# Batch 0 of a fused attention kernel: its first 256 tokens with 256 keys side by side, new first fetches, and a new order

## The chip, the cores and the metric

The kernel runs on one core of one Trainium2 chip. The metric is the device time of one execution in microseconds (us). Three runs of the kernel before took 471.76, 472.86 and 473.77 us; the median is 472.86. Lower is better.

The engines of a core are named as in the profile: PE is TensorE with its matmuls and PEld its weight loads, DVE is VectorE, ACT is ScalarE, POOL is GpSimd, and SP is the engine that does nothing here but issue transfers (DMAs). Each engine takes its own list of instructions in order; between engines there are semaphores.

## The reference

Two attentions stand one behind the other. The first has 8 heads of 64, a causal window of 128 keys and a bias that falls with the distance; its output, 512 wide, is the input of a mixture of four attention experts, of which each token uses the two with the highest gate.

```python
# q, k, v: (8 batches, 8 heads, 576 tokens, 64)
rel = pos[:, None] - pos[None, :]
bias = slopes[:, None, None] * (-np.abs(rel))
mask = (rel >= 0) & (rel < 128)
scores = np.where(mask, q @ k.T / 8 + bias, -1e9)
x = (softmax(scores) @ v)              # -> (8, 576, 512)

logits = x @ w_gate                    # 4 experts, the best two of each token
for e in range(4):
    q, k, v = x @ wq[e], x @ wk[e], x @ wv[e]
    a = softmax(causal(q @ k.T / 8))   # full causal, 576 x 576
    out += (weight of e) * (a @ v @ wo[e])
```

## The kernel before

**Tiling.** Tokens stand in blocks of 128 (four, and a tail of 64), heads in pairs. A batch has four pairs; `g` counts pairs over all batches, so batch 0 has g = 0 to 3. For a pair the first attention computes scores with the tokens on partitions (`products`, L435), adds the bias table `tbt` and takes the row's minimum of the negated scores in one DVE instruction (`softmax_block`, L288; in the trace CUSTOM_DVE_ANT_0, in the order below ISA), takes the exponential with a running sum on ACT (`exp_block`, L292), divides by the sum on POOL or ACT (`normalise`, L470: a reduce and a reciprocal on DVE and one scaling for each block), transposes the probabilities on PE (`half_t`, L511), copies them from PSUM (`evac`, L261, or `split`, L559) and multiplies them with the values (`half_pv`, L534).

**The wrap.** Block 0 has 128 keys. Every later block sees 256 keys, of which each row uses 128 in a staircase. So its scores are computed as two halves of 64 rows with 192 keys each, and `wrap` (L457, COPY_PREDICATED on DVE) folds them into 128 columns: where the mask `mkt` is set, the score of the key 128 places further on replaces the one that the row doesn't use. After the transposes `split` multiplies the folded probabilities with the two masks of `tmt` and so lays them out for 256 keys again.

**Halves of batch 0.** At the start nothing is there to overlap with, so the four pairs of batch 0 are done in halves (`half_units`, L1121): x = 0 is the first 256 tokens (blocks 0 and 1) of all four pairs, x = 1 the rest. `fetch` (L328) brings q and k of the first 256 tokens of a pair (two transfers of 128 KB, one for each half of the partitions, into tiles named w_90 and w_91 in the lists below), and later the rest; `fetch_v` (L360) brings the values `vt`. All of these are issued by SP. The tables `tbt`, `idt` (identity for transposes), `tmt` and `mkt` are issued by ACT (L1094 to L1098).

**The mixture.** Its matmuls keep accuracy by splitting each operand into a rounded part and a rest: weights WH and WL, inputs xT as a high and a low tile. `wload` (L931) fetches a chunk `in_wall` of 772 columns, `wprep` (L946) rounds it to WH (POOL) and subtracts to WL (DVE or POOL); `vproj` (L665) and `qkproj` (L734) do three matmuls for each of four chunks: high x high, high x WL, low x WH. In the trace these are the matmuls with `wx,WH`, `wx,WL` and `WH,wx`; `wx` tiles hold the first attention's output, four of them for batch 0, one per pair.

**Order and buffers.** No code line runs at once: every call is recorded in a list. `plan` (L199) puts the list in the order that a table of numbers (`ORDER`, L38) gives, which also chooses between alternatives (ACT or DVE for a copy, POOL or ACT for a scaling, DVE or POOL for a subtraction) and inserts filler matmuls on a zero tile (`QJm`). `place` (L158) then gives each tile a buffer from its pool. So all instructions have the line of the last loop, L1189, in the trace, and tiles appear by buffer: `w` and `wx` in SBUF, `ps` in PSUM. A copy out of PSUM, for example, is recorded with both engines as alternatives:

```python
    def evac(dst, src, n=0):
        nc.any(("scalar", "copy", (dst, src), None), ("vector", "tensor_copy", (dst, src), None))
```

The program starts at L1093: zero tile, the first table, `fetch(0, 1, 0)`, the other tables, then pairs 1 to 3, the values and the weights.

## Time and profile before

| | |
|---|---|
| median of three runs | 472.86 us |
| the profiled execution | 473.2 us, its span 471.4 us |
| granted clock of PE, mean | 0.998 |
| PE busy | 462.7 us (98% of the span) |
| PEld, DVE, ACT, POOL busy | 403.8, 409.3, 370.5, 222.7 us |
| transferred | 44.99 MB, 95 GB/s over the span |
| chain of waits that ended last | PE 84%, DMA 5%, SP's issues 3%, DVE 3%, ACT 2% |

How to read it: a share is an average over stages. PE is busy nearly all the time, so elsewhere than at the start (and at the end) another engine matters only where PE waits for it. PE's busy time contains the filler matmuls, which do no work for the result. A list entry of a float32 matmul appears twice in PE's timeline, since it runs in two passes; one of the rounded type appears once.

### The profile page before, as it was taken

The numbers are of one execution on the slowest core, as the hardware profiler recorded it, in microseconds if no ns is written. First come the engines' busy times: TensorE is split into PE (matmuls) and PEld (weight loads), VectorE is DVE, ScalarE is ACT, GpSimd is POOL, SyncE is SP. The second block draws the span as 40 slices with busy tenths as digits, with TensorE's granted clock in tenths as the row PEclk, the third lists the DMA queues.
The fourth block names the chain that finished last, engine by engine and source line by source line (L and its number), as shares of the span: only waits on it lengthen the run. The fifth ranks groups of instructions, "written<-read, shape, count | busy, mean of one in ns | idle before, by whom it ended". The sixth has DMA issues, their size and how long they took to land.

```text
span 471.4 us, 17542 instructions
## 1 busy us (share of the span) xinstructions
PE 462.7 (98%) x6380; PEld 403.8 (86%) x6380; DVE 409.3 (87%) x1894; ACT 370.5 (79%) x1409; POOL 222.7 (47%) x464
## 2 busy tenths in 40 slices
PE   7999999999999999999999999999999999999996
PEld 5788999897889789797898987898789897899775
DVE  6999999979998998879989798798999979966852
ACT  5968879989978688796989798897976959833952
POOL 4833968183916346261470907426263623561430
PEclk9999999999999999999999999999999999999999
DMA  7899410345320653150441281602731030300033
GB/s 202 266 221 246 112 52 1 77 103 141 108 80 0 139 142 117 29 140 1 115 129 37 80 189 39 180 2 61 205 121 38 3 86 2 120 1 1 3 113 112
DMA packets 29862, 44.99 MB, mean 95 GB/s; under 512 B 9424, under 2 KB 15824, under 8 KB 29776
## 3 DMA queue, kind: packets, MB, share of 16 engines
q1 hardware_dynamic: 29040, 43.42, 34.0%
q8 instruction: 50, 0.82, 0.8%
q10 hardware_dynamic: 736, 0.46, 0.4%
q14 instruction: 36, 0.29, 0.2%
HBM read 34.42 MB, written 9.44 MB: 93 GB/s over the span
## 4 chain that ended last, share of the span: by engine, by line
PE 84%; DMA 5%; SPq 3%; DVE 3%; ACT 2%; POOL 1%; issue 1%; DVEq 0%
PE ps L1189 84%; DMA w<-in_hd 4%; SPq L1189 3%; DVE w L1189 2%; ACT w L1189 2%; POOL w L1189 1%; DMA w<-in_wall 1%; DVE ps L1189 1%; DVE WL L1189 0%; DVE ALm L1189 0%; ACT AHm L1189 0%; DVE mr L1189 0%; DVE nm L1189 0%; POOL QJm L1189 0%; DVE ALTm L1189 0%
## 5 line engine op out<-in xcount | busy, mean ns | idle before, releaser
L1189 ACT COPY w<-ps 128x256 f32<-128x256 f32 (+2 forms) x232 | 92.4, 443 | 29.8 <-PE ps L1189 21.3
L1189 PE MATMUL ps<-wx,WH 128*128 128x288 f32 (+2 forms) x512 | 110.4, 300 | 0.0
L1189 ACT ACTIVATE w<-w,nm 128x128 f32<-128x128 f32 x252 | 98.9, 397 | 7.3 <-DVE nm L1189 5.8
L1189 POOL TENSOR_SCALAR w<-w,mr,w 128x256 f32<-128x256 f32 (+3 forms) x128 | 78.2, 622 | 43.2 <-DVE mr L1189 24.1
L1189 POOL TENSOR_SCALAR w<-w,r 128x128 f32<-128x128 f32 x177 | 64.6, 378 | 68.3 <-PE ps L1189 25.4
L1189 PEld LDWEIGHTS ps<-wx,WH 128*128 128x128 f32 x512 | 83.2, 190 | 1.5 <-issue 0.3
L1189 ACT ACTIVATE w<-w,mnm 128x512 f32<-128x512 f32 (+3 forms) x128 | 71.2, 558 | 10.0 <-DVE mnm L1189 9.4
L1189 DVE TENSOR_TENSOR w<-ps,tmt 128x768 f32<-128x768 f32 (+3 forms) x96 | 72.5, 770 | 3.3 <-PE ps L1189 2.2
L1189 DVE CUSTOM_DVE_ANT_0 w<-ps,tbt 128x128 f32<-128x128 f32 x288 | 71.7, 283 | 1.1
L1189 PE MATMUL ps<-wx,WL 128*128 128x288 f32 (+2 forms) x256 | 71.9, 298 | 0.0
L1189 PE MATMUL ps<-WH,wx 128*128 128x260 f32 x288 | 61.5, 285 | 0.0
L1189 PE MATMUL ps<-w 64*64 64x192 f32 (+3 forms) x1256 | 58.6, 304 | 2.3 <-DMA w<-in_hd 1.7
L1189 PE MATMUL ps<-idt,w 64*128 64x64 f32 (+1 forms) x1152 | 58.6, 230 | 1.0 <-POOL w L1189 0.9
L1189 PEld LDWEIGHTS ps<-idt,w 64*128 64x128 f32 (+1 forms) x1152 | 47.4, 139 | 11.0 <-issue 3.4
L1189 PE MATMUL ps<-w,vt 64*64 64x192 f32 (+3 forms) x1344 | 56.3, 283 | 0.0
L1189 PEld LDWEIGHTS ps<-w,vt 64*64 64x64 f32 (+1 forms) x1344 | 50.0, 133 | 5.7 <-DVE r L1189 0.6
L1189 DVE COPY_PREDICATED ps<-mkt,ps 128x128 f32<-128x128 int32 (+2 forms) x160 | 49.2, 329 | 5.4 <-PE ps L1189 5.0
L1189 PEld LDWEIGHTS ps<-w 64*64 64x64 f32 (+1 forms) x1256 | 44.0, 134 | 8.6 <-DMA w<-in_hd 2.7
L1189 DVE CUSTOM_DVE_ANT_0 w<-ps,mtt 128x256 f32<-128x256 f32 (+2 forms) x96 | 49.8, 551 | 0.8 <-PE ps L1189 0.4
L1189 PEld LDWEIGHTS ps<-WH,wx 128*128 128x128 f32 x288 | 48.0, 189 | 0.8 <-issue 0.3
L1189 ACT ACTIVATION_READ_ACCUMULATOR w<-w,nm 128x1 f32 x252 | 48.6, 193 | 0.0
L1189 PE MATMUL ps<-w,w 128*64 128x64 f32 (+4 forms) x576 | 48.0, 319 | 0.0
(111 smaller groups left out, 947.5 us busy)
## 6 DMA issues: line engine op xcount, KB each, us to landing
w<-in_hd SPq DMA_DIRECT2D x56, 288.0 KB, 4.6
vt<-in_vd SPq DMA_DIRECT2D x28, 320.0 KB, 3.7
out<-w SPq DMA_DIRECT2D x31, 256.0 KB, 2.5
w<-in_hd SPq DMA_DIRECT2D x14, 128.0 KB, 3.5
w<-in_hd SPq DMA_DIRECT2D x56, 32.0 KB, 3.7
w<-in_wall SPq DMA_DIRECT2D x4, 386.0 KB, 6.6
out<-w SPq DMA_DIRECT2D x8, 128.0 KB, 3.3
vt<-in_vd SPq DMA_DIRECT2D x4, 192.0 KB, 3.8
```

The source lines that it names most:

```text
L1189: getattr(getattr(tc.nc, e), m)(*a, **k)
```

## The change

The change does six things, all in batch 0, and then gives a new order table.

1. **First 256 tokens without the wrap.** For x = 0, `first_blocks` computes block 0 with 128 keys and block 1 with 256 keys side by side (matmuls of 128 and 256 columns instead of 128 and 192), one softmax instruction of 128 and one of 256 columns, and one exp of each for a head. There is no COPY_PREDICATED. The bias comes from a new table `FT` with a causal part and the part for the 128 keys before; it lies in the buffer `KKm`, which the mixture uses only later, and is made from `tbt` by two DVE and four POOL operations. `first_norm` scales the two widths. `half_t` makes six transposes for a pair instead of four and copies them in two plain copies of 384 columns, without `split`; each pair has its own buffers.
2. **First fetches on two queues.** The two first transfers of all four pairs are now recorded first of all, one on SP and one on ACT.
3. **Tables later.** `tmt` and `mkt[:, P:]` move from ACT to SP, recorded behind the weight chunks.
4. **Weights in pieces.** `wprep` rounds and subtracts each of the four chunks in two pieces of 512 and 260 columns.
5. **Low weights last.** In the first half of batch 0's projections (`terms`) the four WL matmuls of an accumulation come behind the eight with WH.
6. **A new `ORDER`**, nearly every number of it. It is the one that also moves work in the rest of the program, transfers on SP among it. Its rows say nothing to a reader, so only a line of each stands here.

The filler matmuls go from 16 to 14. The last loop is L1213 in the changed kernel.

```diff
-    "c-pmi4OAT2b!Jz++w~r*8dX`{p6;D)A8^2i7{-v$Ss23%*pPq+){p}Z*f0SHZ192&4rIZB2_%p}299A2UKB$tIZ`ZqL;{W&ix?*0fCDFJ1`@Oj8`u>yQY<"
+    "c-pmC4^(7Vd7t<0H*@duUNSG4m&~Ly%EZA!!zfs2K_P-d3uZ8of&~j6IEA>R5aEP1V4*?<1!XH(IAznNvIb6<(_IB!n%&CklCoy0;DHDgDi}z?LWN|hOT$"
...
     def fetch(g, m, x):
...
-            for x in range(g, g + m):
-                a = hd[0, NP_ - 1 - x]
...
-                for j in range(2):
...
-                    nc.sync.dma_start(v2[D * j : D * j + D, 1 - x % 2, :, :n], src)
+            for j, e in enumerate((nc.sync, nc.scalar)):
...
+                e.dma_start(v2[D * j : D * j + D, z, :, :n], src)
...
+    def first_blocks(g, ss, q, k, tb):
+        nm, sm, pt = state[g, 0]
+        for i in range(2):
+            n = P + P * i
+            for h in range(2):
+                d = slice(D * h, D * h + D)
+                for y in range(2):
+                    m = P * i + D * y
+                    nc.tensor.matmul(
+                        ss[h][D * y : D * y + D, P * i : P * i + n], q[h][d, m : m + D], k[d, :n], start=True, stop=True
+                    )
+        for h in range(2):
+            for i in range(2):
...
+                softmax_block(a, v, bias, nm[:, c : c + 1], P + P * i)
+                exp_block(None, v, nm[:, c : c + 1], sm[:, c, 0:1], P + P * i)
+
+    def first_norm(g):
...
+            scl(v, v, r[:, c : c + 1])
...
     def half_t(g, x):
...
-            evac(w[:, : 4 * P].rearrange("p (h n) -> p h n", h=2)[:, :, :P], t[:, 0:2, :], 2 * P)
-            split(diag_pair(w, 1, 1, P), t[:, 2:4, :], P)
+            for h in range(2):
+                t = ps_t.tile([P, 4, P], F32, tag="t", name=f"tA{g}_{h}")
+                for k in range(3):
+                    nc.tensor.transpose(t[:, k, :], pt[:, 3 * h + k, :], idt)
+                evac(w[:, 3 * P * h : 3 * P * h + 3 * P].rearrange("p (a n) -> p a n", n=P), t[:, :3, :])
...
+    def terms(late):
+        return sorted(((c, j) for c in range(4) for j in range(3)), key=lambda z: late and z[1] == 2)
...
     def wprep(c):
         if c < 4:
...
+            for f in (slice(0, 4 * P), slice(4 * P, NW)):
+                w, hi, lo = wst[c][:, f], WH[:, NP_ - 1 - c, f], WL[:, NP_ - 1 - c, f]
+                rnd(hi, w)
+                ssub(lo, w, hi.bitcast(F32))
+            return
...
-    fetch(0, 1, 0)
+    for g in range(4):
+        fetch(g, 1, 0)
     nc.scalar.dma_start(idt, ident)
-    nc.scalar.dma_start(tmt, tm)
-    nc.scalar.dma_start(mkt[:, P:], mk[:, P:])
...
+    nc.vector.tensor_scalar(FT[:, 3, :, 0, :], tbt[:, 3, 0:3:2], -1.0e6, NEG, op0=ALU.is_ge, op1=mul)
+    nc.vector.tensor_tensor(FT[:, 3, :, 0, :], FT[:, 3, :, 0, :].bitcast(F32), tbt[:, 3, 1:4:2], add)
+    nc.gpsimd.tensor_scalar(FT[:, 3, :, 1, :], tbt[:, 3, 0:3:2], 1.0, 0.0, op0=mul, op1=add)
+    for p in (2, 1, 0):
+        nc.gpsimd.tensor_scalar(FT[:, p], FT[:, 3].bitcast(F32), float(4 ** (3 - p)), 0.0, op0=mul, op1=add)
...
     for c in range(1, 4):
         wload(c)
+    nc.sync.dma_start(tmt, tm)
+    nc.sync.dma_start(mkt[:, P:], mk[:, P:])
```

Three places of the lists follow, before and then after.

**ACT at the start**, from its first instruction. `hd` is the input with q and k, ACT_TABLE_LOAD loads the table for exp, and an ACTIVATE is an exp of one block.

```order
L1189 DMA tbt<-in_tb 128x640
L1189 DMA idt<-in_ident 128x128
L1189 DMA mkt<-in_mk 128x64
L1189 DMA tmt<-in_tm 128x256
L1189 ACT_TABLE_LOAD
L1189 ACTIVATE w_82,sm_115<-w_82,nmA_132 128x128 [waits DVE_49] x4
L1189 ACTIVATE w_82,sm_116<-w_82,nmA_134 128x128 [waits DVE_49] x4
```

```order
L1213 DMA tbt<-in_tb 128x640
L1213 DMA w_90<-in_hd 64x2x256 x2
L1213 DMA w_91<-in_hd 64x2x256
L1213 DMA idt<-in_ident 128x128 [waits DMAHW0_49]
L1213 DMA w_91<-in_hd 64x2x256 [waits DMAHW2_49]
L1213 ACT_TABLE_LOAD
L1213 ACTIVATE w_82,sm_115<-w_82,nmA_132 128x128 [waits DVE_49] x2
L1213 ACTIVATE w_82,sm_115<-w_82,nmA_132 128x256 [waits DVE_49] x2
```

Three of the four first fetches now stand ahead of `idt`, the fourth waits with a semaphore behind it, and the table load follows them; `mkt` and `tmt` are gone from here.

**DVE, from the end of the first softmaxes into those of the second block.** `r` tiles are reciprocals of row sums, `wx` the outputs of the first attention, ISA with two outputs is a softmax instruction, and `sm` holds the sums. Before, the reciprocal of the second block of pair 0 (`r_4_141`):

```order
L1189 TENSOR_REDUCE r_4_141<-sm_115 128x5 [waits Activation_49,Pool_49]
L1189 TENSOR_TENSOR wx_78<-ps_69,wx_78 128x256 [waits Activation_49]
L1189 RECIPROCAL r_4_141<-r_4_141 128x5 [waits DVE_49]
L1189 COPY_PREDICATED ps_70<-mkt,ps_70 128x2x128
L1189 TENSOR_TENSOR w_92<-ps_76,tmt 128x2x2x128 [waits Activation_49]
L1189 ISA w_82,nmB_142<-ps_70,tbt 128x128 [waits DVE_49]
L1189 ISA nmB_142 128x1
L1189 ISA w_82,nmB_142<-ps_70,tbt 128x128
L1189 ISA nmB_142 128x1
L1189 TENSOR_TENSOR WL<-w_87,WH 128x772 [waits DMAHW4_49,Pool_49]
```

After, the reciprocals of the third and fourth pair's first block (`r_0_137`, `r_0_139`), and some rows later that of the second block of pair 0:

```order
L1213 TENSOR_REDUCE r_0_137<-sm_115 128x4 [waits Activation_49]
L1213 ISA w_82,nmA_138<-ps_74,KKm 128x256 [waits Pool_49]
L1213 ISA nmA_138 128x1
L1213 TENSOR_TENSOR WL<-w_84,WH 128x260 [waits DMAHW3_49,Pool_49]
L1213 ISA w_82,nmA_138<-ps_73,KKm 128x256
L1213 ISA nmA_138 128x1
L1213 RECIPROCAL r_0_137<-r_0_137 128x4 [waits DVE_49]
L1213 CAST wx_77<-ps_72 128x256 [waits PE_49]
L1213 TENSOR_TENSOR wx_77<-ps_72,wx_77 128x256 [waits DVE_49]
L1213 TENSOR_REDUCE r_0_139<-sm_116 128x4 [waits Activation_49]
L1213 RECIPROCAL r_0_139<-r_0_139 128x4 [waits DVE_49]
```

```order
L1213 COPY_PREDICATED ps_71<-mkt,ps_71 128x64
L1213 TENSOR_TENSOR WL<-w_85,WH 128x512 [waits DMAHW1_49,Pool_49]
L1213 ISA w_82,nmB_142<-ps_70,tbt 128x128
L1213 ISA nmB_142 128x1
L1213 TENSOR_REDUCE r_4_141<-sm_115 128x5 [waits Activation_49]
L1213 RECIPROCAL r_4_141<-r_4_141 128x5 [waits DVE_49]
L1213 TENSOR_TENSOR wx_79<-ps_73,wx_79 128x256 [waits Activation_49]
```

Before, the 772 columns of WL on DVE stand behind the reciprocal of pair 0's second block; now a piece of 260 stands ahead of the last two reciprocals of the first block, and a piece of 512 ahead of the reciprocal of pair 0's second block.

**SP in the middle of the program**, where the tiles for the pairs of a later batch are fetched (near 270 us in the trace of before). A tile `w` of q and k takes five transfers; `vt` are values.

```order
L1189 DMA w_86<-in_hd 64x1152 [waits PE_49,DMAHW0_49,Activation_49,Pool_49]
L1189 DMA w_88<-in_hd 64x2x64 [waits DMAHW1_49]
L1189 DMA w_89<-in_hd 64x128 [waits DMAHW2_49]
L1189 DMA w_86<-in_hd 64x2x576 [waits DMAHW3_49]
L1189 DMA w_86<-in_hd 64x64 [waits DMAHW4_49]
L1189 DMA w_89<-in_hd 64x1152 [waits DMAHW5_49]
L1189 DMA vt_283<-in_vd 128x640 [waits DMAHW6_49]
L1189 DMA w_88<-in_hd 64x128 [waits DMAHW7_49]
L1189 DMA w_88<-in_hd 64x2x576 [waits PE_49,DMAHW0_49,Activation_49,Pool_49]
L1189 DMA w_86<-in_hd 64x2x64 [waits DMAHW1_49]
L1189 DMA w_89<-in_hd 64x2x576 [waits DMAHW2_49]
L1189 DMA w_86<-in_hd 64x128 [waits DMAHW3_49]
```

```order
L1213 DMA w_84<-in_hd 64x2x576 [waits PE_49,DMAHW4_49,Activation_49,Pool_49]
L1213 DMA w_87<-in_hd 64x1152 [waits PE_49,DMAHW5_49,Activation_49,Pool_49]
L1213 DMA w_84<-in_hd 64x128 [waits DMAHW6_49]
L1213 DMA w_84<-in_hd 64x2x64 [waits DMAHW7_49]
L1213 DMA w_84<-in_hd 64x1152 [waits DMAHW0_49]
L1213 DMA w_87<-in_hd 64x128 [waits DMAHW1_49]
L1213 DMA w_84<-in_hd 64x64 [waits DMAHW2_49]
L1213 DMA w_87<-in_hd 64x64 [waits DMAHW3_49]
L1213 DMA w_87<-in_hd 64x2x576 [waits DMAHW4_49]
L1213 DMA w_87<-in_hd 64x2x64 [waits DMAHW5_49]
L1213 DMA vt_292<-in_vd 128x640 [waits DMAHW6_49,PE_49]
```

Before, the transfers of w_86, w_88 and w_89 and one `vt` are mixed behind the first wait on other engines; now the ten rows behind the first such wait belong to w_84 and w_87 alone.

## Rows read from the trace of the kernel before

**Rows 1.** Windows of the span: busy us of each engine, clock, DMA share, GB/s
```profile
5.00:10.00 5.00, 4.03 (x64) 2.50 (x62) 3.90 (x31) 3.27 (x17) 1.20 (x3) 1.00 0.87 229
10.00:15.00 5.00, 4.41 (x50) 3.37 (x50) 4.86 (x33) 5.00 (x24) 4.02 (x11) 1.00 0.99 300
...
100.00:400.00 300.00, 298.71 (x4299) 261.55 (x4298) 271.26 (x1254) 248.68 (x949) 138.52 (x300) 1.00 0.32 87
```

**Rows 2.** PE's timeline, start: start us, us, operation, count, [idle before, releaser]
```profile
1.30 3.57 PE L1189 MATMUL ps<-QJm 128*128 128x256 f32 x15 [1.30 <-DVE ps L1187]
4.81 3.69 PE L1189 MATMUL ps<-w 64*64 64x128 f32 x52
...
10.12 0.44 PE L1189 MATMUL ps<-idt,w 128*128 128x128 f32 x2 [0.42 <-POOL w L1189]
...
16.79 0.49 PE L1189 MATMUL ps<-wx,WH 128*128 128x256 f32 x2
...
22.23 0.59 PE L1189 MATMUL ps<-w 128*128 128x192 f32 x2 [0.44 <-DVE w L1189]
```

**Rows 3.** The same timeline where PE does not wait
```profile
15.03 1.52 PE L1189 MATMUL ps<-w,vt 128*64 128x256 f32 x16
16.48 0.55 PE L1189 MATMUL ps<-idt,w 128*128 128x128 f32 x3
...
17.23 0.64 PE L1189 MATMUL ps<-wx,WH 128*128 128x256 f32 x4
17.71 0.52 PE L1189 MATMUL ps<-wx,WL 128*128 128x256 f32 x3
...
25.05 1.53 PE L1189 MATMUL ps<-w 64*64 64x192 f32 x32
26.51 0.77 PE L1189 MATMUL ps<-idt,w 128*128 128x128 f32 x5
27.04 0.36 PE L1189 MATMUL ps<-wx,WH 128*128 128x256 f32 x1
```

**Rows 4.** Chain of waits, start: start us, us, what
```profile
5.45 0.60 SPq L1189
```

**Rows 5.** Timeline of all engines, start: rows of PE's loads, ACT and DVE
```profile
2.93 1.28 ACT L1189 ACT_TABLE_LOAD   x1 [2.93 <-issue]
...
6.73 0.40 ACT L1189 ACTIVATE w<-w,nmA 128x128 f32<-128x128 f32 x1 [2.51 <-DVE nmA L1189]
...
8.94 0.52 PEld L1189 LDWEIGHTS ps<-w 64*64 64x64 f32 x12 [0.80 <-DMA w<-in_hd]
...
19.54 2.28 DVE L1189 TENSOR_TENSOR WL<-w,WH 128x772 fp32r<-128x772 f32 x1
```

**Rows 6.** Groups by shape, ACT: operation xcount | busy us, mean ns | idle before
```profile
L1189 ACT COPY w<-ps 128x512 f32<-128x512 f32 x99 | 56.1, 590 | 16.2 <-PE ps L1189 15.4
...
L1189 ACT COPY w<-ps 128x256 f32<-128x256 f32 x76 | 26.4, 377 | 8.9 <-PE ps L1189 3.9 <-DVE lg L1189 3.8 <-DMA out<-w 0.7
...
L1189 ACT ACTIVATE w<-w,mnm 128x256 f32<-128x256 f32 x32 | 16.1, 504 | 1.7 <-DVE mnm L1189 1.4
...
L1189 ACT ACTIVATE w<-w,nmA 128x128 f32<-128x128 f32 x16 | 6.2, 390 | 2.5 <-DVE nmA L1189 2.5
```

**Rows 7.** The same of DVE
```profile
L1189 DVE COPY_PREDICATED ps<-mkt,ps 128x128 f32<-128x128 int32 x64 | 17.7, 288 | 3.7 <-PE ps L1189 3.5
...
L1189 DVE TENSOR_TENSOR w<-ps,tmt 128x512 f32<-128x512 f32 x4 | 2.7, 669 | 0.0
```

**Rows 8.** PE's timeline, two later waits
```profile
284.45 0.60 PE L1189 MATMUL ps<-w 64*64 64x128 f32 x10 [0.67 <-DMA w<-in_hd]
...
339.83 1.37 PE L1189 MATMUL ps<-w 64*64 64x192 f32 x30 [0.55 <-DMA w<-in_hd]
```

**Rows 9.** Chain of waits, 270 to 290 us
```profile
270.00 0.22 POOL QJm L1189
...
277.66 6.74 DMA w<-in_hd
```

265 lines of the change are left out of this document (128 added, 137 removed).

## The prediction

> **What bounds the kernel now.** I read the stages first, then PE's own timeline. Between 100 and 400 us PE is busy for 298.7 of the 300 us [rows 1], 1.3 idle; there only fewer or cheaper matmuls would help, or the end of those few waits. The other place is the start. There DVE and ACT are as full as PE later is: 4.86 and 5.00 of the 5 us from 10 to 15 [rows 1], and PE, which takes its list in order, waits for their softmax. It computes its first score at 4.81, its first transpose only at 10.12, its first projection matmul (wx,WH) at 16.79, and the last wait of the start ends at 22.23 [rows 2]. From there its list runs almost without a gap, so the time is: matmul work, plus what PE stands idle before 22.23, plus the few waits later. The change touches all three.
>
> **Prices on PE.** Prices are start to start, from stretches in which PE does not wait [rows 3]. Sixteen 64x192 score matmuls (x32, each runs twice) take 25.05 to 26.51: 0.091 each, so I take 0.061 for 128 columns and 0.121 for 256. Five transposes take 26.51 to 27.04: 0.106 each. The weighted sums (w,vt) of two head pairs take 15.03 to 16.48: 1.45. Four projection matmuls of 256 columns take 17.23 to 17.71: 0.12 each.
>
> **Work added.** The first block of scores of each of the four pairs (g = 0 to 3) goes from four matmuls of 128 and four of 192 columns to four of 128 and four of 256: 16 x (0.121 - 0.091) = +0.48. The first block now has three probability tiles per head instead of two: 24 transposes for 16, +8 x 0.106 = +0.85. One filler matmul in the middle goes (-0.12); the other stood ahead of the first score, where PE waits anyway. Together **+1.2 us**, certain, since PE is the bound.
>
> **Work taken from DVE and ACT.** DVE loses eight wraps of 0.29 and four splits of 0.67 [rows 7], 5.0 us; it gains four copies of 384 columns, by ACT's copies of 256 and 512 between 0.38 and 0.59 each [rows 6], so 1.9, and more pieces of the low weights. ACT's sixteen exps become eight of 128 at 0.39 and eight of 256 at 0.50 [rows 6]: 7.1 instead of 6.2, and four of the 384 copies are its own. So DVE is relieved and ACT, full already, is not. Costed at nothing: the first tables FT (two operations on DVE, four on POOL), which run between the table's landing near 3.1 and the first score; if that cover fails, the first block waits about 0.5. Also at nothing: tm and mk, which are now issued on SP behind three weight chunks; their first readers are the tail and the split of the second block, which stand behind all of the first.
>
> **When ACT starts.** Before, the eight first fetches left SP one after the other, the last at 5.45 [rows 4], and PE had its data at 8.94 [rows 5], 3.5 us later. Half of them now leave ACT. But ACT's list is in order: the fourth of them waits for an earlier transfer, and the table load of 1.28 us, which ran at 2.93 [rows 5], stands behind it. An earlier transfer lands 3.3 to 3.5 after an issue at 0.7 to 1.2, so 4.1 to 4.6; plus 0.6 for the issue and 1.28 for the load, ACT is ready at 5.9 to 6.4. I take 6.3, against a first exp at 6.73 [rows 5].
> The Trainium skill, "DMA: Bandwidth & Descriptors", section "Issuing engines are not separate DMA queues", speaks against a gain here: transfers from any issuer share the same 16 engines, and a second issuer only saves issue time. The DMA share of 0.87 between 5 and 10 us [rows 1] leaves little room and so bears it out. By the row, issue time is what spaces the first fetches (0.65 each); by the rule alone the first exp would stay at 6.7 and the sum below would be 0.4 higher.
>
> **The start, walked.** The new PE list has all the weighted sums of the first block ahead of the first projection matmul, where the old one had two of four pairs. So the question is when the fourth pair's sums are done. ACT has before them: 7.1 of exps, four scalings (three of 256 at 0.50, one of 0.39: 1.9), four copies (1.9), one cast (0.4) and two exps of the next block (0.8): 12.1. From 6.3 that is 18.4, and half of 1.45 for the last pair's sums gives 19.1. DVE can hold it up: the reciprocal and the last score block of the third and fourth pair stand behind a 260-column piece of the low weights, 0.77 long by the 2.28 that 772 took [rows 5]. With all of it, 20.0. I take **19.5**.
> Now the idle time. Two matmuls of the tail and the second block's first scores (C) are in both lists up to their first projection matmul and cancel. Before, at 16.79: 2.43 of scores, 16 transposes 1.70, sums 1.45, a filler 0.12 make 5.70, so 11.09 - C idle. From 16.79 to 22.23: 20 projection matmuls 2.40, five transposes 0.53, sums 1.45 make 4.38 of 5.44, so 1.06 more: 12.15 - C. After, at 19.5: scores 2.91, 24 transposes 2.54, sums 2.90 make 8.35, so 11.15 - C. Then 19 projection matmuls run, 2.3 us, and the second block's transposes of pair 0 follow. They need a reciprocal that on DVE stands behind a 512-column piece (1.5 by the same row): a wait from 0 to 1.5, I take 0.7. So 11.85 - C, **-0.3 us**. The bounds are -2.2 (ACT ready at 5.9, copies at 0.38: sums done at 18.3, no wait) and +1.5 (20.0, the 0.5 of FT on top, and the wait of 1.5).
>
> **Later waits.** Two waits of the long middle end with a transfer, 0.67 and 0.55 us of PE's idle time [rows 8]. The first is one of SP's list: a buffer came free at 270.2, eleven transfers for three tiles and one of vt were issued behind it one by one, and the last of them, issued at 277.66, landed 6.74 later [rows 9], when PE needed it. In the new list the same place holds ten transfers for two tiles, and the first tile is complete with the seventh: at 0.65 each, the last part leaves two to five issues earlier, 1.3 to 3.2 us. That would cover this wait, if the buffer comes free as early. I take 1.0 of the two waits as gone. Bounds: -2.0 (all the 1.3 idle of [rows 1] and what the modelled ends of matmuls hide beside it) and +0.6 (both stay, one more of the kind comes).
>
> **Sum.** +1.2 - 0.3 - 1.0 = -0.1. The profiled execution took 473.2 with its span of 471.4, 0.3 above the median of 472.86; the difference goes on the median: **472.8**.
>
> **Rivals.**
> *DVE decides the start (slower).* The pieces of the low weights run on DVE beside POOL's own, at 2.28 for 772 columns [rows 5]; three pieces, 1284 columns together, now stand on DVE among the reciprocals and wraps for which ACT and PE wait. If they run at that rate in every place, and the fourth pair's sums end at 20.5 and pair 0's second block waits 1.5, the start costs +1.5 and the sum is 1.2 + 1.5 + 0 = +2.7 with the old transfer waits kept, 475.5; with one more, 476.1. It decides from about 1 us more idle time at the start, if the transfers give nothing. For it: DVE busy 4.86 of 5 us there [rows 1]. Against: the 5.0 us that DVE loses. Chance 0.18.
> The Trainium skill, "SBUF — State Buffer", section "SBUF: two separate sides", says that VectorE with two inputs from SBUF and GpSimd lock each other out for a whole instruction; the long piece in [rows 5] is what that would look like.
> *The start comes clear (faster).* ACT begins at 5.9, DVE never stands in its way, the sums end at 18.3, no wait follows: -2.2, and the later waits go: -2.0. With +1.2: 469.9. For it: DVE's relief, weights that land earlier. Against: it wants both at their bounds. Chance 0.20.
> *The two queues do nothing.* The first fetches land no earlier, the first exp stays at 6.7: 473.2. Chance 0.10, no change.
> *PE falls to the lower clock.* The fillers of the start took 0.24 for 256 columns [rows 2], twice the 0.12 of [rows 3]: the pace of the 1.2 GHz level against that of 2.4, and the granted clock from 5 us on reads 1.00 [rows 1]. Its gaps after the first scores were each under 0.9 before. Now its first scores end near 8.2, and the first transposes, 3.4 after the first exp before [rows 2, 5], come later for the wider exps and scalings: about 10.5, a gap of some 2.3. If the clock falls there, the sums of the first two pairs take 2.9 for 1.45: +1.4, 474.2. Chance 0.12, no change.
> The Trainium skill, "TensorE: Matmul & The Clock Gate", section "HAM oscillation — how this bites in real kernels", describes this, a matmul after a wait for data that starts at the low clock; the gaps of this trace show no case of it.
>
> **How the numbers follow.** The forecast has the remaining 0.40. What a measurement of this kernel can tell from no change is about 0.5%, 2.4 us: 470.5 to 475.2. The forecast, the queues and the clock lie inside: 0.62; faster 0.20, slower 0.18. The range leaves out the outer half of each side case: 469.9 to 475.8.
>
> **What would show it.** First exp at 6.3 and PE's first projection matmul at 19.5, after a start with few waits behind it: right. First exp above 6.7: the queues did nothing. Projection matmuls from 20.5 on, with PE waiting for DVE before pair 0's transposes: the slower rival. Before 18.5: the faster one. Transposes at 0.2 each near 11 us: the clock. PE idle above 1.3 us between 100 and 400, with waits for a transfer: the margin did nothing. The prediction is wrong if a stage that I took as unchanged, the long middle or the end, moves by more than 2 us.

## The result, and the profile after

The changed kernel took 475.61 us (median of four runs, 475.33 to 475.80) against 472.93 for the kernel before beside it: ratio 1.0058, 95% interval 1.0036 to 1.0080. It is 2.7 us slower. The time lies inside the forecast's range, at its upper edge, but it is more than a measurement's uncertainty away from no change, and no change was forecast. The profiled execution took 475.64, its span 473.7.

The busy times of the whole page, which answer to the table of before (PE 462.7, PEld 403.8, DVE 409.3, ACT 370.5, POOL 222.7):

```profile
PE 465.4 (98%) x6386; PEld 404.6 (85%) x6386; DVE 408.5 (86%) x1903; ACT 370.9 (78%) x1401; POOL 223.6 (47%) x469
```

The windows that answer to [rows 1], same columns:

```profile
5.00:10.00 5.00, 2.86 (x52) 1.72 (x48) 3.37 (x23) 4.43 (x16) 3.67 (x7) 1.00 1.06 257
10.00:15.00 5.00, 4.35 (x31) 3.26 (x32) 3.54 (x18) 3.64 (x15) 4.29 (x9) 0.68 1.08 318
100.00:400.00 300.00, 299.61 (x4302) 260.93 (x4301) 270.06 (x1262) 245.46 (x932) 139.47 (x302) 1.00 0.33 87
```

The long middle did what was forecast, by this view: PE's idle time between 100 and 400 us fell from 1.29 to 0.39. The start did not. From 10 to 15 us the granted clock is 0.68, from 5 to 10 PE is busy for 2.86 us instead of 4.03. PE's timeline of the start, which answers to [rows 2, 3]:

```profile
5.92 2.22 PE L1213 MATMUL ps<-w 64*64 64x256 f32 x40 [0.28 <-DVE nmA L1213]
10.65 0.87 PE L1213 MATMUL ps<-w 64*64 64x128 f32 x12 [2.51 <-DMA w<-in_hd]
11.45 2.50 PE L1213 MATMUL ps<-idt,w 128*128 128x128 f32 x12
13.88 2.18 PE L1213 MATMUL ps<-w,vt 128*64 128x256 f32 x16
...
21.01 2.76 PE L1213 MATMUL ps<-wx,WH 128*128 128x256 f32 x21
```

There is a gap of 2.51 before 10.65, ended by a first fetch. Behind it twelve transposes take 2.43 (11.45 to 13.88), where [rows 3] give 0.106 each, and the sums of two pairs 2.10 where [rows 3] give 1.45. The first projection matmul is at 21.01, forecast at 19.5. Windows of one microsecond show the clock itself (same columns as above):

```profile
11.00:12.00 1.00, 1.00 (x14) 0.61 (x7) 0.19 (x2) 1.00 (x5) 0.96 (x3) 0.92 1.21 254
12.00:13.00 1.00, 1.00 (x7) 1.00 (x6) 0.72 (x4) 0.62 (x4) 1.00 (x3) 0.50 1.03 289
13.00:14.00 1.00, 1.00 (x7) 0.67 (x7) 0.95 (x6) 0.02 (x1) 1.00 (x2) 0.50 1.06 368
14.00:15.00 1.00, 1.00 (x7) 0.62 (x8) 1.00 (x6) 1.00 (x4) 0.41 (x1) 0.50 1.02 359
```

In this column 1.00 is the 2.4 GHz level and 0.50 the 1.2 GHz level. The gap comes from ACT's list. In the timeline of all engines the fourth first fetch is issued on ACT at 4.92, the table load and the first exp follow:

```profile
4.92 0.61 ACTq L1213 DMA_DIRECT2D w<-in_hd  x1
...
5.56 1.28 ACT L1213 ACT_TABLE_LOAD   x1 [5.56 <-DMA w<-in_hd]
...
6.86 0.40 ACT L1213 ACTIVATE w<-w,nmA 128x128 f32<-128x128 f32 x1
```

The fetch waits for an earlier transfer, as the order showed, but the wait ends at 4.92 and not at 4.1 to 4.6. So its data come at 10.6. The table load stands behind it, and the first exp comes at 6.86 instead of 6.3, later than the 6.73 of before [rows 5].

So far this reads like the rival in which PE falls to the lower clock, with a late fetch on top. But the same kernel, run again beside the experiments, had a trace without any of it (rows of PE, then of ACT, from its timeline):

```profile
4.59 4.69 PE L1213 MATMUL ps<-w 64*64 64x128 f32 x64
9.36 2.75 PE L1213 MATMUL ps<-idt,w 128*128 128x128 f32 x12
12.04 1.52 PE L1213 MATMUL ps<-w,vt 128*64 128x256 f32 x16
...
19.33 2.90 PE L1213 MATMUL ps<-wx,WH 128*128 128x256 f32 x21
...
4.30 0.61 ACTq L1213 DMA_DIRECT2D w<-in_hd  x1
...
4.94 1.28 ACT L1213 ACT_TABLE_LOAD   x1 [4.94 <-DMA w<-in_hd]
...
6.24 0.40 ACT L1213 ACTIVATE w<-w,nmA 128x128 f32<-128x128 f32 x1
```

The fetch leaves at 4.30, there is no gap, the clock is 1.00 throughout the start, and the first projection matmul stands at 19.33, near the 19.5 of the forecast. Yet the median of its six runs was 475.59, ratio 1.0064 (1.0049 to 1.0078). The accident at the start is not what makes the kernel slower.

The timed runs say so too, by the mean granted clock of PE over each run's whole span. Some 3 us at 0.50 in 473 us take about 0.003 off it. The five traces of this study in which the clock fell at the start have means of 0.994 to 0.996, all other traces 0.998 to 1.000, and no run lies between. The mean doesn't say where in a run the clock fell, so it stands here as a sign of the same event. Medians in us, number of runs in brackets:

| kernel | mean clock 0.998 to 1.000 | mean clock 0.994 to 0.996 |
|---|---|---|
| changed | 475.58 (3) | 475.64 (1) |
| changed, again | 475.50 (5) | 475.73 (1) |
| before, beside the first runs of "Mending the start" | 472.10 (7) | 472.54 (5) |
| before, beside "changed, again" | 472.11 (22) | 473.49 (7) |
| new order from 66 to 213 us only (below) | 473.97 (5) | 475.45 (4) |

So the low clock is no mark of the change: it shows in 2 of 10 runs of the changed kernel and in 20 of 85 of the kernel before. Runs of the kernel before that have it take 0.4 to 1.4 longer. In the runs without it the changed kernel stands 3.4 above the kernel before (475.50 and 472.11).

**A table by place.** To see where the time is, I cut every trace at the same matmuls of PE's list. The first cut is the start of the 104th transposing matmul (with `idt`; the 112th where the new start adds eight). It lies in these rows of PE's timeline, of before and of after:

```profile
64.90 1.06 PE L1189 MATMUL ps<-idt,w 64*128 64x64 f32 x17
```

```profile
67.04 0.98 PE L1213 MATMUL ps<-idt,w 64*128 64x64 f32 x17
```

The second cut is 396 such matmuls later. Between the two, every kernel of this study has the same 1560 matmuls of the list, so this stretch differs by PE's waiting alone. Worked out from the start times, in us:

| trace | to the first cut | between | second cut to the end | first cut to the end |
|---|---|---|---|---|
| before | 65.63 | 147.34 | 258.43 | 405.8 |
| before, again | 65.40 | 147.22 | 257.29 | 404.5 |
| changed | 67.69 | 148.23 | 257.78 | 406.0 |
| changed, again | 66.44 | 148.33 | 258.13 | 406.5 |

The forecast had +0.9 for the start (+1.2 - 0.3) and -1.0 for the rest. The first pair of traces has +2.06 and +0.24, the second +1.04 and +1.96. So the start comes out near the forecast in the trace without gap and low clock, and 1 us worse in the one with both; the rest is 1.2 to 3.0 us worse than forecast. The experiments take these apart.

### The profile page after: what moved, and what is told of

It reads as the page before. It is cut to its first block, busy times and chain, and to the rows that moved or that the text cites. A ratio compares the mean times of both kernels' runs of the same rounds, so it can differ in the third digit from the quotient of the medians.

```text
span 473.7 us, 17579 instructions
## 1 busy us (share of the span) xinstructions
PE 465.4 (98%) x6386; PEld 404.6 (85%) x6386; DVE 408.5 (86%) x1903; ACT 370.9 (78%) x1401; POOL 223.6 (47%) x469
## 4 chain that ended last, share of the span: by engine, by line
PE 62%; DVE 3%; SPq 1%; ACT 1%; POOL 1%; DMA 1%; issue 1%; DVEq 0%; ACTq 0%
PE ps L1213 62%; DVE w L1213 1%; SPq L1213 1%; ACT w L1213 1%; POOL w L1213 1%; DVE ps L1213 1%; DMA w<-in_hd 1%; DVE lg L1213 0%; DVE r L1213 0%; DVE KKm L1213 0%; DVE wx L1213 0%; DVE QLm L1213 0%; ACT KKm L1213 0%; DVE mr L1213 0%; DVE nm L1213 0%
## 5 line engine op out<-in xcount | busy, mean ns | idle before, releaser
L1213 ACT COPY w<-ps 128x512 f32<-128x512 f32 (+4 forms) x232 | 93.6, 447 | 32.5 <-PE ps L1213 21.4
L1213 PE MATMUL ps<-wx,WH 128*128 128x288 f32 (+2 forms) x512 | 108.5, 300 | 0.0
L1213 ACT ACTIVATE w<-w,nm 128x128 f32<-128x128 f32 x252 | 98.8, 395 | 6.4 <-DVE nm L1213 5.9
L1213 POOL TENSOR_SCALAR w<-w,mr,w 128x128 f32<-128x128 f32 (+3 forms) x128 | 79.1, 629 | 52.0 <-DVE mr L1213 26.2
L1213 POOL TENSOR_SCALAR w<-w,r 128x128 f32<-128x128 f32 (+1 forms) x164 | 59.1, 373 | 55.5 <-PE ps L1213 15.6
L1213 PEld LDWEIGHTS ps<-wx,WH 128*128 128x128 f32 x512 | 82.0, 189 | 3.0 <-issue 0.9
L1213 ACT ACTIVATE w<-w,mnm 128x256 f32<-128x256 f32 (+3 forms) x128 | 71.2, 560 | 13.6 <-DVE mnm L1213 13.3
L1213 DVE TENSOR_TENSOR w<-ps,tmt 128x768 f32<-128x768 f32 (+2 forms) x92 | 69.4, 773 | 1.0 <-PE ps L1213 0.5
L1213 PE MATMUL ps<-wx,WL 128*128 128x288 f32 (+2 forms) x256 | 69.8, 298 | 0.0
L1213 DVE CUSTOM_DVE_ANT_0 w<-ps,tbt 128x128 f32<-128x128 f32 x272 | 68.0, 282 | 1.0 <-PE ps L1213 0.3
L1213 PE MATMUL ps<-idt,w 64*128 64x64 f32 (+1 forms) x1160 | 61.2, 232 | 0.4
L1213 PE MATMUL ps<-w 64*64 64x192 f32 (+4 forms) x1256 | 57.0, 304 | 2.8 <-DMA w<-in_hd 2.5
L1213 PEld LDWEIGHTS ps<-idt,w 64*128 64x128 f32 (+1 forms) x1160 | 49.9, 140 | 10.8 <-issue 2.8
L1213 PE MATMUL ps<-WH,wx 128*128 128x260 f32 x288 | 58.2, 285 | 0.0
L1213 PE MATMUL ps<-w,vt 64*64 64x192 f32 (+4 forms) x1344 | 56.2, 284 | 0.0
L1213 PEld LDWEIGHTS ps<-w,vt 64*64 64x64 f32 (+1 forms) x1344 | 49.7, 134 | 5.7 <-issue 1.4
L1213 PEld LDWEIGHTS ps<-w 64*64 64x64 f32 (+1 forms) x1256 | 42.9, 133 | 9.4 <-DMA w<-in_hd 2.9
L1213 DVE CUSTOM_DVE_ANT_0 w<-ps,mtt 128x512 f32<-128x512 f32 (+2 forms) x96 | 49.8, 549 | 1.1 <-PE ps L1213 1.1
L1213 ACT ACTIVATION_READ_ACCUMULATOR w<-w,nm 128x1 f32 x252 | 48.2, 191 | 0.0
L1213 PE MATMUL ps<-w,w 128*64 128x64 f32 (+4 forms) x576 | 48.0, 319 | 0.0
L1213 DVE COPY_PREDICATED ps<-mkt,ps 128x256 f32<-128x256 int32 (+2 forms) x152 | 45.9, 330 | 1.8 <-PE ps L1213 1.3
L1213 DVE COPY w<-ps 128x256 f32<-128x256 f32 (+4 forms) x82 | 37.6, 471 | 10.7 <-PE ps L1213 9.9
```

The lines of the kernel that those rows point to most:

```text
L1213: getattr(getattr(tc.nc, e), m)(*a, **k)
```

## The experiments

Two theories. **Start**: the late fourth fetch, DVE's piece of WL and the low clock make the kernel slower. **Rest**: the new order of the compute work behind the start costs what the transfers give, and more. Ratios stand against the kernel before in the same job.

### Mending the start

The fourth first fetch goes ahead of `idt` in ACT's list:

```diff
 DMA w_90<-in_hd 64x2x256 x2
-DMA w_91<-in_hd 64x2x256
+DMA w_91<-in_hd 64x2x256 x2
 DMA idt<-in_ident 128x128
-DMA w_91<-in_hd 64x2x256
 ACT_TABLE_LOAD
```

> The changed kernel with two rows of ACT's list exchanged: the last first fetch (the second half of pair 3) goes ahead of the transfer of idt. Theory A, the late fetch: in the changed kernel it was issued at 4.92 and ended PE's wait of 2.51 us at 10.65; the granted clock read 0.50 from 12 to 15, where 3.4 us of work ran at half speed, 1.7 us. Issued at 3.2 it lands near 7.6, PE's wait is under 1.5 us, the clock stays at 1.00, the first projection matmul comes at 18.5 to 19.5 instead of 21.01, and the time is 472.8 to 473.8. Theory B, ACT and DVE: the exps still begin at 6.86, because the table load stands behind the same waits, so the transposes come no earlier than now; then PE waits as long, for scalings, the clock falls all the same, and the time stays at 475 to 476.

Measured: 474.81, ratio 1.0059 (1.0042 to 1.0075). PE's wait, then DVE's piece of WL and POOL's instruction beside it:

```profile
9.86 2.88 PE L1213 MATMUL ps<-idt,w 128*128 128x128 f32 x12 [0.96 <-POOL w L1213]
...
13.47 1.38 DVE L1213 TENSOR_TENSOR WL<-w,WH 128x260 fp32r<-128x260 f32 x1
...
13.28 1.28 POOL L1213 TENSOR_TENSOR WL<-w,WH 128x512 fp32r<-128x512 f32 x1
```

The gap is 0.96 now, the granted clock stays at 1.00 in the start, the projections begin at 19.95, and the kernel is as slow as before the mending. The load of the exp table now stands behind `idt`, which left at 5.32, and the first exp comes at 6.99. Here the 260 columns of WL took 1.38. In the changed kernel's trace the same instruction started after POOL's had ended, and took 0.42:

```profile
13.14 1.27 POOL L1213 TENSOR_TENSOR WL<-w,WH 128x512 fp32r<-128x512 f32 x1
...
14.65 0.42 DVE L1213 TENSOR_TENSOR WL<-w,WH 128x260 fp32r<-128x260 f32 x1
```

So the piece that the forecast priced at 0.77 costs 0.42 alone and 1.4 beside POOL. The Trainium skill, "SBUF — State Buffer", section "SBUF: two separate sides", says that VectorE with two inputs from SBUF and GpSimd take a shared port in turn, a whole instruction each; these rows agree.

With `idt` on SP as well:

```diff
-    nc.scalar.dma_start(idt, ident)
+    nc.sync.dma_start(idt, ident)
```

> As the run before, and idt is issued by SP behind the first fetches, so that ACT has no wait for an earlier transfer's place ahead of its table load: load at about 3.8, first exp at 5.9 instead of 6.86. Theory A with ACT as the next limit: the whole chain of scalings and transposes comes 0.8 to 0.9 earlier than in e1_fetch_before_idt, 472.0 to 472.9. If the first exp was held by DVE's softmax or by the fetches instead, the two runs are equal within 0.3.

Measured: 474.20, 1.0045 (1.0028 to 1.0061). The same answer, if a little smaller. The table load has ended at 5.16 here, and the first exp waits for DVE's softmax:

```profile
6.35 0.40 ACT L1213 ACTIVATE w<-w,nmA 128x128 f32<-128x128 f32 x1 [1.19 <-DVE nmA L1213]
```

So without the waits in ACT's list the first exp came at 6.35. Twenty filler matmuls in the gap ahead of the fourth pair's scores, everything else as changed:

```diff
+MATMUL ps<-QJm 128x256 x20
```

> The changed kernel with 20 filler matmuls of 256 columns ahead of pair 3's scores, in PE's wait for the late fetch; all transfers as they were. They take 2.4 us at 0.12 each, the wait has 2.51. Theory A, with the clock as its larger part: the fetch still lands at 10.6, but the granted clock stays at 1.00 from 11 to 15, the twelve transposes take 1.3 instead of 2.50 and the first projection matmul comes about 1.7 earlier, 473.6 to 474.2. If the wait itself is the loss and the clock only goes along, the time stays at 475.3 to 476. If ACT and DVE set the pace behind it, the sums come at the same time as now in spite of the clock, 475.6.

Measured: 475.37, 1.0067 (1.0049 to 1.0084). PE's timeline:

```profile
10.08 2.65 PE L1215 MATMUL ps<-QJm 128*128 128x256 f32 x20
12.66 0.88 PE L1215 MATMUL ps<-w 64*64 64x128 f32 x16
13.47 1.53 PE L1215 MATMUL ps<-idt,w 128*128 128x128 f32 x12
14.93 2.07 PE L1215 MATMUL ps<-w,vt 128*64 128x256 f32 x16
16.93 1.53 PE L1215 MATMUL ps<-w 64*64 64x192 f32 x32
...
21.95 2.28 PE L1215 MATMUL ps<-wx,WH 128*128 128x256 f32 x17
```

PE does not stand idle ahead of the late data, and the clock stays at 1.00: twelve transposes take 1.46 (13.47 to 14.93) where the changed kernel's trace had 2.43. So the low clock cost up to 0.97 there. The sums take 2.00 here at the full clock (14.93 to 16.93), so the 2.10 of the changed kernel's trace need not be the clock's. The fillers end late, at 12.66, and the projections begin at 21.95: a low clock is avoided, and nothing is won.

The fetch mended and the 260-column piece of WL moved behind the last reciprocal and an output of the first block:

```diff
 ISA w_82,nmA_138<-ps_74,KKm 128x256
-TENSOR_TENSOR WL<-w_84,WH 128x260
 ISA w_82,nmA_138<-ps_73,KKm 128x256
...
 TENSOR_TENSOR wx_78<-ps_71,wx_78 128x256
+TENSOR_TENSOR WL<-w_84,WH 128x260
```

> e1_fetch_before_idt, and on DVE the piece of 260 low weights goes from ahead of pair 3's last softmax to behind pair 3's reciprocal. In e1 this piece took 1.38 us, beside POOL's own piece of 512 columns, where it took 0.42 in the changed kernel; the last softmax, the reciprocal of pair 2, POOL's scalings and the transposes at 15.99 stood behind it. Theory D, DVE's piece is what bounds the mended start: the transposes of pair 2 come at 15.0 and the first projection matmul at 18.9 to 19.2 instead of 19.95; the time is 0.7 to 1.0 below e1's. If the start is bound by ACT's exps (10 to 15 us full), it moves by 0.3 or less.

Measured: 475.29, 1.0068 (1.0053 to 1.0082). The clock fell in its profiled execution (0.69 from 10 to 15 us), but its other five runs have mean clocks of 0.998 to 1.000. Their median is 475.11, 3.1 above the kernel before without the fall (472.01); the same difference was 2.6 before the move (474.69 and 472.10). So the move gained nothing.

Two transposes for a head instead of three, with the fetch mended. This leaves out a part of the computation:

```diff
-                for k in range(3):
+                for k in range(2):
```

> e1_fetch_before_idt with two probability tiles for each head of the first block instead of three: eight transposes fewer, and the eight copies behind them of 256 columns instead of 384; the weighted sums take a wrong tile, so this leaves out part of the computation. My prediction put +0.85 on these transposes as certain, since PE is the bound. If it is, the time is 0.8 to 1.0 below e1's. If PE has waits at the start that hide them (1.7 us of idle time between 9 and 17 in e1), it is 0.4 below or less, what the shorter copies give.

Measured: 475.54, 1.0070 (1.0058 to 1.0082). Eight transposes fewer, nothing gained. In its profiled execution the scores (60 rows) took from 6.00 to 11.58, and the first cut came at 67.96, so the start was held by something else. The +0.85 of the forecast is neither shown nor refuted.

### Cutting the order in two

The order table was cut at one place of PE's list, just before the first cut of the table above. New start, old rest:

```diff
-ORDER = new
+ORDER = new up to PE's matmul 591, then old
```

> The changed kernel up to the point where 591 matmuls are in PE's list (67.7 us in its trace; the kernel before has the same work behind it at 65.6), from there the old order. Theory C, the new order gains nothing behind the start: from that point to the end the changed kernel takes 406.0 us and the kernel before 405.8, so this run is at 475.0 to 475.8, with the old waits for a transfer near 284 and 340 back. If the new order's margin on transfers does give the 1.0 us that I put on it, this run is at 476.3 to 476.8. If the new order costs something in the middle, it is at 474.5 or below.

Measured: 473.90, 1.0037 (1.0023 to 1.0050). All seven runs have a mean clock of 0.996; in the trace it fell at 11.6 us, behind a gap of 1.71 ahead of the late data. The opposite, the kernel before with its own start and the new order behind it:

```diff
-ORDER = old
+ORDER = old up to PE's matmul 584, then new
```

> The other half of e4: the kernel before up to 584 matmuls (65.6 us in its trace), from there the new order. In e4 the old order took 403.9 us from that point to the end, in the changed kernel the new one took 406.0, in the kernel before the old one 405.8, of which 1.3 is idle time before two late transfers. Theory C2: the new order has no late transfers but makes PE wait for ACT (4.5 us of PE's weight loads in the changed kernel, 1.6 in the kernel before, 1.9 in e4), so it takes 406 behind any start: this run is within 0.7 of the kernel before. Theory C3: what the rest takes is the accident of where the start ends, not of the order: then the new order behind the old start may take 404, 1.5 to 2 us faster than the kernel before.

Measured: 473.70, 1.0038 (1.0024 to 1.0052). The last kernel contains no part of the change but the order behind the start, and still has two thirds of the loss. By place: the new rest takes 406.6 behind the old start (406.0 and 406.5 behind the new one), the old rest 403.8 behind the new start. So both halves cost time: by the ratios +1.7 for the start and +1.8 for the rest. That is more than the +2.7 to +3.0 of both together, and the start's share is the less certain one: here it has the low clock in every run, in the changed kernel in 2 of 10. Without it the start cost +1.04 in the second trace of the changed kernel.

The mended start of the runs above with the old rest:

> e6 up to the point of e4, from there the old order. If the parts add up: e4's distance of +1.6 to the kernel before, less 0.6 for the fetch and 0.8 for the piece of low weights, +0.2: within 0.6 of the kernel before. If the later waits for transfers come back with the earlier start, as in the kernel before, +1.5 to +2.

Measured: 473.46, 1.0026 (1.0014 to 1.0038). Its four runs without the low clock have the same median, 473.46, which is 1.45 above the kernel before without it (472.01). In its profiled execution `idt` was late in its turn, and the clock fell (0.71 from 10 to 15 us):

```profile
10.45 1.52 PE L1214 MATMUL ps<-idt,w 128*128 128x128 f32 x6 [1.13 <-DMA idt<-in_ident]
```

### The start without waits

The mended start, `idt` on SP, the first pair's last scores ahead of the first softmax's wait, and eight fillers ahead of the first transposes, with the old rest:

```diff
+MATMUL ps<-QJm 128x256 x8
```

> e7_mended_start_old_rest with three changes at the start: idt is issued by SP as in e2, the matmuls of 256 columns of pair 0 stand ahead of DVE's first softmax (PE waited 0.7 us for it between 5.3 and 6.0), and eight filler matmuls stand between the last scores and the first transposes, where PE was idle 1 us and the granted clock fell to 0.50 behind it in e6 and e7, not in e1. Theory E, the pace of PE decides the start: the clock stays at 1.00 from 10 to 15, the first projection matmul comes at 19.0 to 20.0 instead of 21.3 to 21.7, and the time is 0.8 to 1.5 below e7, within 0.6 of the kernel before. If the start is bound by the exps and scalings and PE's pace only goes along, within 0.4 of e7.

Measured: 472.63, 1.0010 (0.9994 to 1.0026). PE's timeline:

```profile
9.97 1.29 PE L1216 MATMUL ps<-idt,w 128*128 128x128 f32 x6
...
19.07 2.83 PE L1216 MATMUL ps<-wx,WH 128*128 128x256 f32 x21
```

The projections begin at 19.07 and the first cut comes at 65.81, 0.2 to 0.4 behind the two traces of before. None of the twelve runs shows the low clock, nor do the twelve of another kernel with this start (with grouped transfers, below), in whose trace the first cut came at 66.70. The new start can be had at little cost when PE is kept busy in it; it gives nothing.

### The rest: transfers and compute order

The kernel before with one part of the new order: the five transfers of one tile stand together, first in their batch, at two places of SP's list. The first, near 270 us:

```diff
 DMA w_86<-in_hd 64x1152
-DMA w_88<-in_hd 64x2x64
-DMA w_89<-in_hd 64x128
 DMA w_86<-in_hd 64x2x576
 DMA w_86<-in_hd 64x64
+DMA w_86<-in_hd 64x2x64
+DMA w_86<-in_hd 64x128
+DMA w_88<-in_hd 64x2x64
+DMA w_89<-in_hd 64x128
```

> The kernel before with SP's list changed at two places alone: the five transfers of the tile that PE waited for at 284.45 stand together at the head of their batch of transfers, and so do those of the tile that it waited for at 339.83. This is the margin on transfers by itself. My prediction put 1.0 us on these waits. If that is right, both waits are gone from the trace and the time is 0.7 to 1.3 below the kernel before, and this kernel is faster than both. If a wait that goes comes back at the next engine (as 4.5 us of waits for ACT stand in the changed kernel), the waits are gone and the time is within 0.4.

Measured: 471.33, 0.9989 (0.9977 to 1.0001); in a second job:

> The kernel of e9_old_tiles_together once more, on another chip: e9 was 0.87 below the kernel before, its interval [0.9977, 1.0001] just reached no change. If the margin on transfers is worth about 1 us, it is again 0.5 to 1.2 below, and faster than both kernels; if e9 was a lucky draw, within 0.4.

Measured: 471.10, 0.9976 (0.9962 to 0.9990). That is 0.9 and 1.1 us less than before, and faster than both kernels. The window of the first one's long middle, columns as in [rows 1]:

```profile
100.00:400.00 300.00, 299.92 (x4306) 262.43 (x4305) 272.89 (x1262) 249.26 (x951) 138.68 (x302) 1.00 0.33 88
```

PE idles 0.08 of the 300 us. In the runs without the low clock the gain is 0.9 in both jobs (471.25 for 472.11, 471.05 for 471.95). It stands behind the second cut, where the two places are: 256.6 and 256.5 in the two traces, against 258.4 and 257.3 in those of before. So the term of -1.0 for the later waits had the right size and place, and what costs the rest its time is not the transfers. The busy start and the grouped transfers, together:

> e10_start_kept_busy with the two batches of transfers of e9 in its old rest. If what e9 gained adds up with the mended start (e10 was 0.4 above the kernel before), 0.3 to 0.8 below the kernel before. If the gain of e9 hangs on where the start ends (e10's trace shows no wait for a transfer), it is at e10's distance, +0.2 to +0.7.

Measured: 472.29, 1.0001 (0.9987 to 1.0014). Beside the 1.0010 of the busy start alone this is no difference that can be told. The traces of both show no wait of PE for a transfer behind the start: with the new start the waits that the grouping takes away weren't there.

The new order from 213 us on only, and from 66 to 213 us only:

> The kernel before up to 213 us of its trace, from there the new order. In e5 the new order from 65.6 on cost 1.7 us. If that is many small waits all along, this run has a bit over half of it, +0.8 to +1.1. If it stands at one place in the first half, within 0.3 of the kernel before; if in the second half, +1.5 or more.

> The complement of e11: the kernel before with the new order from 65.6 to 213 us alone, then the old one. e5 (new from 65.6 to the end) cost 1.7, e11 (new from 213 to the end) nothing. If the parts add up, this run is 1.4 to 2.0 above the kernel before. If the loss needs the new order's later part as well, within 0.6 of it.

Measured: 472.44, 0.9998 (0.9990 to 1.0006), and 474.34, 1.0045 (1.0027 to 1.0063). So the loss that shows in the time comes with the order between 66 and 213 us: +2.0 without the low clock (473.97 for 471.95). The new order from 213 us on is free only as a whole, for it contains the grouped transfers: behind the second cut its one trace takes 257.6, some 1.1 more than the old order with its tiles together (256.5 and 256.6). In the kernel with the new order from 66 to 213 us, 1.1 to 1.2 of the loss is PE's waiting in that stretch itself, since the matmuls are the same: 148.45 against 147.2 to 147.3. Behind the second cut it takes 258.39 against 257.29 and 258.43 for before; there the old order is back, and I didn't follow it further. An estimate that prices each matmul of PE's timeline at its undisturbed rate puts 0.8 to 0.9 of the new order's loss at about 147 to 155 us and 0.45 just behind 213.

The first of the two places, from the timeline of all engines, in the kernel with the old start and the new rest:

```profile
150.78 0.17 DVE L1189 TENSOR_REDUCE r<-sm 128x5 f32<-128x10 f32 x1 [1.83 <-POOL w L1189]
...
152.32 0.28 DVE L1189 COPY lg<-ps 128x4 f32<-128x4 f32 x3
...
152.57 0.37 ACT L1189 COPY w<-ps 128x256 f32<-128x256 f32 x1 [2.41 <-DVE lg L1189]
...
152.99 0.14 PEld L1189 LDWEIGHTS ps<-idt,w 64*128 64x128 f32 x1 [0.28 <-ACT w L1189]
```

A reduce of DVE waits 1.83 for a scaling on POOL. Behind it in DVE's list stand the copies of `lg`; ACT's copy out of PSUM waits 2.41 for one of them, and a weight load of PE waits for that copy, 0.28. Why the place loses 0.8 where the wait shown is 0.28 the rows don't tell. To try the chain, the reduce and its reciprocal were moved behind the first copy of `lg`:

```diff
-TENSOR_REDUCE r_0_232<-sm_115 128x5
 TENSOR_TENSOR lg_228<-ps_73,w_102 64x4 x2
-RECIPROCAL r_0_232<-r_0_232 128x5
...
 COPY lg_228<-ps_75 128x4
+TENSOR_REDUCE r_0_232<-sm_115 128x5
+RECIPROCAL r_0_232<-r_0_232 128x5
```

> e5_old_start_new_rest with one step of DVE's list moved, near 151 us: the reduce and reciprocal r of a row sum go behind the copy of the gates lg of token block 3. In e5 DVE stood idle 1.83 us ahead of this reduce, which waited for POOL; ACT stood idle 2.41 us for a copy behind it, and PE's transposes waited for the bank that this copy empties. Theory F, the new order's loss is such chains: DVE's idle time ahead of the reduce and ACT's 2.41 shrink to under 1 us, PE gets through this place 0.5 to 0.8 earlier, and the time is 0.4 to 0.8 below e5's distance of +1.7. If PE waits there for something else, the place stays as it is and so does the time.

Measured: 473.63, 1.0035 (1.0020 to 1.0049), beside 1.0038 without it: no difference that can be told. The window of its start, then the timeline of all engines at the place:

```profile
10.00:15.00 5.00, 3.93 (x21) 3.13 (x24) 3.29 (x24) 3.89 (x19) 3.05 (x9) 0.66 0.95 297
```

```profile
151.93 0.46 DVE L1189 TENSOR_TENSOR QLm<-ps,QHm 128x288 fp32r<-128x288 f32 x1 [0.93 <-ACT QHm L1189]
...
152.97 0.15 DVE L1189 COPY lg<-ps 128x4 f32<-128x4 f32 x1
...
153.04 0.15 DVE L1189 TENSOR_REDUCE r<-sm 128x5 f32<-128x10 f32 x1
...
153.49 0.38 ACT L1189 COPY w<-ps 128x256 f32<-128x256 f32 x1 [1.59 <-DVE lg L1189]
```

DVE no longer stands still before the reduce (it waits 0.93 for ACT at another row), ACT's wait is 1.59 for 2.41, no weight load waits for ACT there, and the stretch between the cuts is 0.4 shorter (148.05). This execution had the low clock in the start (0.66), with the old start, and its first cut at 67.03. Six of its ten runs were without it, with a median of 473.38, 1.4 above the kernel before without it (471.95); the same difference was 1.7 in the kernel without the move (473.68 and 472.01). So the move may be worth some 0.2, which these few runs don't settle, and most of the loss has other causes. The link is shown at its place, not in the time.

The second place stands in the changed kernel's trace behind a burst of 65 transposes, PE's weight loads:

```profile
219.64 0.28 PEld L1213 LDWEIGHTS ps<-w,w 128*64 128x64 f32 x4 [0.57 <-ACT w L1213]
220.35 0.65 PEld L1213 LDWEIGHTS ps<-w,w 128*64 128x64 f32 x8 [0.43 <-ACT w L1213]
```

And the kernel before, run again, at the same weight loads, and at the wait of [rows 8] that a transfer ended:

> The kernel before itself, for a second trace. From the place where 104 transposes are done to the end its first trace took 405.8 us, e9 and e13 (the same with two batches of transfers regrouped) 404.2, e4 and e7 (its order behind the new start) 403.7 to 403.8. If the two late transfers near 284 and 340 belong to its order, they are there again, and the stretch is 405.3 to 406.2. If they came by chance in the first trace, they are gone, the stretch is 404.0 to 404.6 and e9 gained nothing in its usual executions.

Measured: 471.73, beside 471.49 of another run of it.

```profile
215.65 0.14 PEld L1189 LDWEIGHTS ps<-w,w 128*64 128x64 f32 x2 [0.28 <-ACT w L1189]
...
216.45 0.85 PEld L1189 LDWEIGHTS ps<-w,w 128*64 128x64 f32 x8 [0.23 <-ACT w L1189]
...
283.30 0.30 PEld L1189 LDWEIGHTS ps<-w 64*64 64x64 f32 x10 [0.25 <-DMA w<-in_hd]
```

ACT ends waits of 1.00 together in the new order, of 0.51 in the old one. The transfer that cost 0.67 in the first trace [rows 8] holds a weight load for 0.25 in this one, the one that cost 0.55 costs 0.25, and the stretch from the first cut to the end is 1.3 shorter (404.5 for 405.8), only 0.3 above the 404.2 with the grouped transfers. So in this execution there was little left for the grouping to gain: what the margin on transfers can give differs from execution to execution, and the 0.9 is a median over many.

> The changed kernel itself, beside the others on the same chip. If its start is what the first trace showed (late fetch, PE idle 2.5 us, clock 0.50 for 3.4 us), the second trace shows it again and the time is 2.2 to 3.2 above the kernel before. If the start goes this way in some executions only, the trace shows another one, and the times spread over more than 1.5 us.

The last one is the changed kernel once more, whose rows stand above.

## Why the forecast was wrong, step by step

- **What bounds the kernel** held: PE is full, and time is gained or lost where it waits.
- **Work added, +1.2.** Not refuted, not isolated. Twelve transposes of the new start took 1.46 where PE doesn't wait, 0.12 each against my 0.106, so +0.1 more for the eight that were added.
- **When ACT starts, 6.3.** It was 6.86 and 6.24 in two executions. My upper bound of 6.4 came from the landing of one earlier transfer between 4.1 and 4.6; the wait for it ended at 4.9 in one execution and by 4.3 in the other. In both the exp began as the table load ended, so ACT's list set it. With `idt` on SP the list was free at 5.16, and the exp came at 6.35, behind DVE: 6.3 was near, but the bound of 5.9 left out DVE's softmax. By the section of the Trainium skill that I weighed against this step, "Issuing engines are not separate DMA queues" in "DMA: Bandwidth & Descriptors", a second issuer saves issue time alone, and the exp would have stayed at 6.7. The two traces don't decide on that, since the order of ACT's list set the exp in both.
- **The start, -0.3.** Near in the trace without the accident: first projection at 19.33 for 19.5, and +1.04 of start for +0.9. The kernel with the mended start and the old rest still lost 1.45 without the low clock.
- **The rival of the lower clock.** Such falls happen and cost about what was put on them (0.97 on the transposes of one trace, 1.5 in the runs of the new order from 66 to 213 us, for 1.4), but they don't make this change slower: they are as frequent in the kernel before (20 of 85 runs) as in the changed one (2 of 10), whose runs with and without them took the same time. Nor does a long gap tell them apart: gaps of 0.95 and 2.51 stood before a fall in two traces, one of 0.96 left the clock at 1.00 in a third, and with the old start it fell behind three waits of 0.45 to 0.59.
- **DVE decides the start.** The time that it forecast, 475.5, was met by luck and not by this mechanism. The piece priced at 0.77 took 0.42 in the changed kernel's trace and 1.38 in the one with the fetch mended, and the kernels were equally slow; moving it away gained nothing.
- **Later waits, -1.0.** Right in size and place with the old start: -0.9 and -1.1 alone. That it is these two waits is only in part shown, since the second trace of before had little of them; and with the new start PE waited for no transfer there.
- **The step that failed** is the sentence "From there its list runs almost without a gap", and with it the rest of the program left out of the sum. I read SP's list of the new order in the middle and took DVE's, ACT's and PE's there for equal, though the table of numbers changes nearly all of them. The runs put +1.7 us on the new order behind the start with its transfers (old start, new rest), where the forecast had -1.0; the part from 66 to 213 us alone costs +2.1. Without what the transfers give, the new order's cost is some +2.5 by an estimate from the traces (406.0 to 406.8 from the first cut on, against 404.2 for the old order with its tiles together). One cue stood in the lists: at the place near 152 us the new one has a reduce that waits for POOL ahead of the copies of `lg` for which ACT waits. Moving that reduce didn't bring the time back, so which waits of the new order make up the loss stays open.
- **PE's idle column misled me twice.** In the forecast 1.3 us idle between 100 and 400 us looked like the most that could be lost or won there. And after, 0.39 idle stood beside a slower middle. A matmul counts as busy until its modelled end, so a late weight load can hide in it. The waits of the weight loads (PEld) over the same 300 us (us in total, times, longest), of before and of after:

```profile
PEld ps L1189 <- ACT w L1189: 1.6, 6, 0.4
...
PEld ps L1189 <- DMA w<-in_hd: 0.8, 1, 0.8
```

```profile
PEld ps L1213 <- ACT w L1213: 4.5, 17, 0.6
```

Those for ACT are three times as many. Their sum is no price either: from 213 us on it grew as well, from 1.1 to 2.3 with the new order there alone, and what that cost can't be parted from what the transfers gave. Why some of them cost PE time and others don't was not settled.
